# Two transformer-like layers on one core: turning the normalised x through DRAM instead of with ACT block copies

## The chip, the core and the metric

The kernel runs on one core of a Trainium2 chip. Its time is the device time of one execution in microseconds (us); of several runs the median is given. The engines are named as in the profile: PE (matrix multiply, with PEld for its weight loads), DVE (vector), ACT (activation), POOL (GpSimd) and SP, which here only issues DMAs.

## The reference

Everything is fp32. x has 2048 rows of 640 features. Two layers follow each other, each an attention block and a dense block, with shared weights:

```python
x = x + A(layernorm(x), wqkv, wo)          # twice, with B after each
x = x + B(layernorm(x), w1, b1, w2, b2)

def A(x, wqkv, wo):                        # 32 heads of 20, linear attention
    q, k, v = split(x @ wqkv)
    phi = lambda t: where(t > 0, t + 1, exp(t)) + 1e-6
    pq, pk = phi(q), phi(k)
    kv, z = einsum("bhsd,bhse->bhde", pk, v), pk.sum(over s)
    return ((pq @ kv) / (pq . z + 1e-6)) @ wo

def B(x, w1, b1, w2, b2):                  # 640 -> 1728 -> 640
    h = relu(x @ w1 + b1)
    return (h * h) @ w2 + b2
```

## The kernel before

The 2048 rows are 16 tiles of 128 rows (P = 128, 640 = D = 5 x 128, DC = 5). Each fp32 operand of a product is split into a high part, rounded by ACT, and a low part, the rest, made by DVE; a product is three matmuls (`mm3`). A matmul contracts over partitions, so the normalised x has to be turned: features onto partitions, rows along the free axis.

**The turn.** `blocks_T` (L370) transposes a 128 x 640 tile on DVE in 32 x 32 blocks, each block in its own place. `blocks_move` (L375) then moves the blocks to their places with 16 ACT copies of 32 partitions by 160 elements (L381). After that the tile is split into high (ACT) and low (DVE), by `xT_split` (L402, lines L130 and L131) in the attention block and by `x_split` (L1289, L1295 and L1297) in the dense block. The same two functions turn the attention's `pq` tiles (`b_ops`). Tiles 0, 1 and 2 of the first layer, and tiles 2 and 3 of each dense block, are turned by PE (`transpose5`).

**The attention loop** (L702) goes over the tiles t. Iteration t projects tile t to k and q (`part`), applies phi (`Phi`: ACT exp L491, DVE L498 and L499), gathers products of x and k of tile t - 1 (`g_part`, `gt_part`), normalises tile t + 2 (`a_apply`) and starts its turn, and splits tile t + 1. `k_post` makes the high and low parts of k (L683, L690) and adds k up on POOL (L687). In the first layer the loop also prepares w1 and w2 (`Prep`): it loads raw units (L265), splits them (L244, L248), and stores the split units to DRAM (L251); the wqkv split is stored as well (L210).

**The start of the first layer.** `FirstLoads` loads the k columns of wqkv in five chunks of 128 features, then the q columns in five more (L205), and splits them (L183 high, L189 low). Matmuls of the first tile (L726) follow chunk by chunk; the last of the q chunks stand in PE's order ahead of the first product of tile 1 (L395), and on ACT the splits of the last two q chunks stand ahead of the split of tile 1 (L130).

**The dense block** (from L1039) goes over four groups g of four tiles; in a group it goes over 14 chunks c of the 1728 hidden features. An iteration is `fc1` of chunk c (15 matmuls, L1064), `act` (ACT relu L1076, DVE L1077 to L1079), and `fc2` of chunk c - 1 (L1114). Beside it run, at places written out by hand, the attention outputs, norms and turns of the next group's tiles: `single` for tiles 4 to 7, `side` with the plans `fast(b)` for tiles 8 to 15. An event at (c, i) stands after tile i of `fc2` in iteration c, one at (c, "post") at the iteration's end. The split w1 and w2 units come back from DRAM through a ring of six buffers (`Units.load_ring`, L304). In the last group the next layer's tiles 0, 1 and 2 are normalised and turned (`side_last`).

**Order of the work.** The order on every engine is the program's order. All DMAs but one are issued by SP, in program order; an issue that waits holds up all behind it. SP's DMAs use eight completion semaphores in turn, so that a DMA is issued once the eighth before it has landed.

## Time and profile before

| | |
|---|---|
| time, median of 3 runs (lowest to highest) | 1351.68 us (1351.64 to 1351.83) |
| profiled execution | its time is its span, 1349.9 us; the page gives no other time for it |
| busy: PE, PEld, DVE, ACT, POOL | 1342.1, 1158.3, 911.7, 770.3, 123.4 us |
| DMA moved | 253.44 MB, mean 188 GB/s |

The span runs from the first instruction to the last; the timed runs hold 1.8 us more, which lies around it. A row of a group ends in "busy, mean of one in ns | idle time before, and what ended it". A row of the timeline begins with the start and the length in us.

### The profile page before, as it was taken

What the parts mean: (1) busy time and instruction counts of PE and PEld (TensorE: products, weight loads), DVE (VectorE), ACT (ScalarE), POOL (GpSimd) and SP (SyncE); (2) the same over time, 40 slices, a digit from 0 to 9 for tenths busy, and PEclk for the clock granted to TensorE, in tenths of its full rate; (3) what the DMA queues carried; (4) which work ended last, traced back from release to release, by engine and by line L of the source; (5) the groups of instructions that cost most, each with busy time, mean ns of one, the idle gap of its engine ahead of it and who ended that gap; (6) DMA issues with size and microseconds to landing.
All of it is one profiled execution on the core that took longest, in us unless ns stands there. A gap on an engine that the chain in (4) does not pass through costs nothing.

```text
span 1349.9 us, 18967 instructions
## 1 busy us (share of the span) xinstructions
PE 1342.1 (99%) x6797; PEld 1158.3 (86%) x6797; DVE 911.7 (68%) x1627; ACT 770.3 (57%) x1932; POOL 123.4 (9%) x174
## 2 busy tenths in 40 slices
PE   9999999999999999999999999999999999999998
PEld 8888998888888888888888899988888888888887
DVE  7888757777777676643467676677778667775323
ACT  5878858676546448411447688494756446464110
POOL 2222210000000000000012232100000000000000
PEclk9999999999999999999999999999999999999999
DMA  6787835574665475387521115156546646644734
GB/s 205 254 301 269 284 86 177 192 275 145 212 237 174 158 292 170 117 327 293 184 98 51 48 40 155 41 206 255 173 157 232 216 150 223 233 167 140 287 125 158
DMA packets 85635, 253.44 MB, mean 188 GB/s; under 512 B 11030, under 2 KB 19606, under 8 KB 84902
## 3 DMA queue, kind: packets, MB, share of 16 engines
q1 hardware_dynamic: 85398, 252.04, 53.7%
q8 instruction: 54, 0.88, 0.3%
q14 instruction: 39, 0.32, 0.1%
q10 hardware_dynamic: 144, 0.20, 0.0%
HBM read 193.50 MB, written 56.03 MB: 185 GB/s over the span
## 4 chain that ended last, share of the span: by engine, by line
PE 92%; DVE 3%; ACT 3%; DMA 1%; issue 1%; POOL 0%; SPq 0%; DVEq 0%; ACTq 0%
PE PS L395 34%; PE PS L1064 28%; PE PS L1114 28%; ACT z L381 2%; PE PS L911 1%; PE PS L924 1%; DMA st<-in_A_wqkv_dram 1%; PE PS L726 0%; DVE bn L352 0%; DVE xr L658 0%; DVE e L498 0%; DVE xTb L131 0%; DMA Mr<-Mc 0%; DVE r L499 0%; PE PS L1128 0%
## 5 line engine op out<-in xcount | busy, mean ns | idle before, releaser
L381 ACT ACTIVATE z<-y 32x160 f32<-32x160 f32 x1424 | 475.8, 334 | 75.2 <-DVE y L372 59.0
L1064 PE MATMUL PS<-xTb,u 128*128 128x512 f32 x1400 | 333.8, 390 | 1.0 <-DVE xTb L131 1.0
L1064 PEld LDWEIGHTS PS<-xTb,u 128*128 128x128 f32 x1400 | 261.6, 188 | 55.0 <-DVE xTb L131 1.5
L395 PE MATMUL PS<-kq,xT 128*128 128x320 f32 (+2 forms) x1575 | 284.4, 334 | 0.4 <-DVE GT L529 0.4
L1114 PE MATMUL PS<-u,h 128*128 128x512 f32 x1120 | 276.8, 390 | 0.0
L395 PEld LDWEIGHTS PS<-kq,xT 128*128 128x128 f32 x1575 | 250.1, 188 | 28.2 <-DVE rl L499 1.0
L1114 PEld LDWEIGHTS PS<-u,h 128*128 128x128 f32 x1120 | 208.5, 188 | 40.8
L1076 ACT ACTIVATE hr<-PS,b1sb 128x512 f32<-128x512 f32 x104 | 71.4, 687 | 297.6 <-PE PS L1064 296.9
L1077 DVE TENSOR_TENSOR hr<-hr 128x512 f32<-128x512 f32 x104 | 71.8, 690 | 217.4 <-ACT hr L1076 216.9
L395 PE MATMUL PS<-kh,xh 128*128 128x512 f32 x480 | 124.6, 393 | 0.0
L491 ACT ACTIVATE e<-PS 128x320 f32<-128x320 f32 (+4 forms) x128 | 53.5, 435 | 101.9 <-PE PS L395 93.5
L356 POOL TENSOR_SCALAR rs<-mv 128x1 f32<-128x1 f32 x64 | 28.0, 438 | 869.6 <-DVE mv L354 869.6
L395 PE MATMUL PS<-uM,pT 128*128 128x320 f32 x648 | 102.6, 309 | 0.7 <-DVE uM L940 0.7
L395 PEld LDWEIGHTS PS<-kh,xh 128*128 128x128 f32 x480 | 87.2, 188 | 15.6 <-DVE kh L690 0.4
L395 PEld LDWEIGHTS PS<-uM,pT 128*128 128x128 f32 x648 | 97.7, 188 | 3.1 <-DVE uM L940 1.2
L498 DVE TENSOR_SCALAR e<-e 128x320 f32<-128x320 f32 (+4 forms) x128 | 41.7, 325 | 80.0 <-ACT e L491 79.7
L1114 PE MATMUL PS<-h,u 128*128 128x512 f32 x280 | 79.0, 390 | 0.0
L1079 DVE TENSOR_TENSOR h<-hr,h 128x512 fp32r<-128x512 f32 x104 | 72.0, 693 | 3.6
L687 POOL TENSOR_TENSOR acc<-acc,r 128x640 f32<-128x640 f32 x30 | 53.8, 1795 | 198.5 <-DVE r L499 198.5
L1114 PEld LDWEIGHTS PS<-h,u 128*128 128x128 f32 x280 | 52.2, 188 | 10.8 <-DVE h L1090 0.4
L1064 PE MATMUL PS<-xTb,uw 128*128 128x512 f32 x240 | 57.0, 389 | 0.0
L499 DVE SCALAR_TENSOR_TENSOR r<-PS,e 128x512 f32<-128x512 f32 (+2 forms) x104 | 51.1, 492 | 5.8 <-ACT e L491 2.4
(126 smaller groups left out, 1353.9 us busy)
## 6 DMA issues: line engine op xcount, KB each, us to landing
u<-kept_w SPq DMA_DIRECT2D x184, 640.0 KB, 4.3
x<-x SPq DMA_DIRECT2D x48, 320.0 KB, 6.3
kept_w<-uprep SPq DMA_DIRECT2D x23, 640.0 KB, 4.9
pqt<-pq SPq DMA_DIRECT2D x32, 320.0 KB, 5.6
x<-xr SPq DMA_DIRECT2D x32, 320.0 KB, 2.4
st<-in_B_w_dram SPq DMA_DIRECT2D x22, 320.0 KB, 5.6
pq<-r SPq DMA_DIRECT2D x20, 320.0 KB
kept_kq<-kq SPq DMA_DIRECT2D x10, 640.0 KB, 5.7
```

The costliest lines, as they stand in the source:

```text
L356: nc.gpsimd.tensor_scalar(rs, mv[:, 1:2], LN_EPS, None, op0=ALU.add)
L381: nc.scalar.activation(zv[j * B32 : (j + 1) * B32, :, i, :], yv[i * B32 : (i + 1) * B32, :, j, :], AF.Copy)
L395: nc.tensor.matmul(ps, a, b, start=first and i == 0, stop=last and i == 2)
L491: nc.scalar.activation(self.e[:, a:b], ps, AF.Exp)
L498: nc.vector.tensor_scalar(e, e, 1.0, PHI_EPS, op0=ALU.min, op1=ALU.add)
L499: nc.vector.scalar_tensor_tensor(out=self.r[:, a:b], in0=ps, scalar=0.0, in1=e, op0=ALU.max, op1=ALU.add)
L687: nc.gpsimd.tensor_tensor(out=acc, in0=acc, in1=r, op=ALU.add)
L1064: nc.tensor.matmul(ps, a[:, d, :], bb[:, d, :], start=d == 0 and i == 0, stop=d == DC - 1 and i == len(seq) - 1,)
L1076: nc.scalar.activation(r, ps, AF.Relu, bias=b1sb[:, c : c + 1])
L1077: nc.vector.tensor_tensor(out=r, in0=r, in1=r, op=ALU.mult)
L1079: nc.vector.tensor_tensor(out=h[:, 1], in0=r, in1=h[:, 0].bitcast(F32), op=ALU.subtract)
L1114: nc.tensor.matmul(ps, l, r, start=first and k == 0, stop=last and k == len(a) - 1)
```

## The change

The turn of x now goes through DRAM. `spread` writes the normalised tile to DRAM with a DMA issued by POOL, and reads it back with four DMAs issued by SP: partition group j (32 partitions) of the tile `z` gets the features 160 j to 160 j + 159, in four blocks of 32 rows. One DVE transpose in 32 x 32 blocks (`turn`), with permuted access patterns, then gives the turned tile, and the 16 ACT copies go. Chunk c of the turned tile holds the features 160 j + 32 c + q on partition 32 j + q, no longer 128 c to 128 c + 127. So the rows of w1 and of wqkv's k and q columns are loaded in the same order, each load in four DMAs of 32 partitions; and where PE or ACT copies still turn x (the first three tiles of layer one, tiles 0 to 3 of each dense block) the normalised tile is written in permuted order. The attention's `pq` tiles keep their copies. In the dense block's plans some places move.

```diff
+JQ = P // B32
+Q = D // JQ
...
 def src_w1(c):
-            return [(v, w1[:, c * P : c * P + n].rearrange("(d p) f -> p d f", p=P))]
+            w = w1[:, c * P : c * P + n]
+            return [
+                (v[j * B32 : (j + 1) * B32], w[Q * j : Q * (j + 1)].rearrange("(d p) f -> p d f", p=B32))
+                for j in range(JQ)
+            ]
...
 class FirstLoads, step:
-                    nc.sync.dma_start(raw, wqkv[c * P : (c + 1) * P, D * (nm == "k") :][:, :D])
+                    for j in range(JQ):
+                        r = Q * j + B32 * c
+                        nc.sync.dma_start(
+                            raw[j * B32 : (j + 1) * B32], wqkv[r : r + B32, D * (nm == "k") :][:, :D]
+                        )
...
+    def spread(src):
+        n = bounce[0] % 8
+        bounce[0] += 1
+        d = dram.tile([P, D], F32, name="xb", tag=f"xb_{n}")
+        nc.gpsimd.dma_start(d, src)
+        z = ftile("z")
+        for j in range(JQ):
+            nc.sync.dma_start(
+                z[j * B32 : (j + 1) * B32].rearrange("p (i f) -> p i f", f=Q),
+                d[:, j * Q : (j + 1) * Q].rearrange("(i q) f -> q i f", q=B32),
+            )
+        return z
+
+    def turn(z):
+        y = ftile("y")
+        nc.vector.transpose(
+            out=y.rearrange("p (c i q) -> p i c q", c=DC, q=B32),
+            in_=z.rearrange("p (i c q) -> p i c q", c=DC, q=B32),
+        )
+        return y
...
 attention loop, iteration t:
-            move(t + 1)
             f.exp(0, ps)
...
                 a_apply(t + 2)
-                yza[t + 2] = blocks_T(xt[t + 2])
+                yza[t + 2] = spread(xt[t + 2])
             f.rest()
             ps = part(t, n0, D if is_late else 1024, bank(XB[1]))
             if t + 1 in yza:
-                xT_split(t + 1, yza.pop(t + 1)[1])
+                xT_split(t + 1, turn(yza.pop(t + 1)))
...
-            move(t + 2, AHEAD)
...
 x_split:
-            v = yzx.pop(t)[1].rearrange("p (c n) -> p c n", c=DC)
+            v = turn(yzx.pop(t)).rearrange("p (c n) -> p c n", c=DC)
...
 single:
-            at(b + 1, "post", lambda: blocks_move(yzx[t], (0, 1)))
+            at(b + 1, "post", lambda: x_spread(t))
-            at(b + 2, "pre", lambda: blocks_move(yzx[t], (2, 3)))
...
 fast(b), the entry "back": stats, apply, spread (moves before), split high, split low, bias
-        [((b, "post"), (b + 1, 0), (b + 1, 1), (b + 2, 0), (b + 2, 1), (b + 2, 3)),
-         ((b + 1, 3), (b + 1, "post"), (b + 2, 0), (b + 2, 4), (b + 3, 0), (b + 3, 1))],
+        [((b, "post"), (b + 1, 0), (b + 1, 2), (b + 2, 0), (b + 2, 1), (b + 2, 3)),
+         ((b + 1, 3), (b + 1, "post"), (b + 2, 0), (b + 3, 0), (b + 3, 1), (b + 3, 2))],
...
 side_last (next layer's tiles 0, 1, 2): spread at c = 7, 8, 11; turn and split of tiles 0, 1 at c = 9, 11
```

More of the change, by code (lines that the diff above doesn't have):

```diff
@@ L382, in blocks_move, with turn_move @@
                     zv[j * B32 : (j + 1) * B32, :, i, :], yv[i * B32 : (i + 1) * B32, :, j, :], AF.Copy
+                )
+    def turn_move(yz, js):
+        if len(yz) == 1:
+            yz.append(ftile("z"))
+        yv = yz[0].rearrange("p (j c q) -> p j c q", c=DC, q=B32)
+        zv = yz[1].rearrange("p (c i q) -> p c i q", c=DC, q=B32)
+        for j in js:
+            for i in range(P // B32):
+                nc.scalar.activation(
+                    zv[j * B32 : (j + 1) * B32, :, i, :], yv[i * B32 : (i + 1) * B32, j], AF.Copy
                 )
@@ L435, in a_stats, with a_apply @@
             ln_stats(("a", t), xt[t])
-    def a_apply(t):
-        if t < NT:
+    def a_apply(t, chunked=False):
+        if t < NT and chunked:
+            raw, xt[t] = xt[t], ftile("xp")
+            ln_apply(("a", t), by_chunk(xt[t]), by_block(raw))
+        elif t < NT:
             ln_apply(("a", t), xt[t], xt[t])
@@ L512, in split_new, with x_natural @@
             return u
+        def x_natural(t):
+            u = xtile("xh")
+            split(by_block(u[:, 0]), by_block(u[:, 1]), by_chunk(xt[t]))
+            return u
         def g_part(t, i):
@@ L787 @@
                 a_apply(3)
[L788 removed]
+                yza[3] = spread(xt[3])
             if early:
[L790 removed]
+                xT_split(2, turn(yz0[2]))
             for _ in range(PREP.get(t, 0) if layer == 0 else 0):
@@ L802 @@
                 fq.rest()
-            xh[t] = split_new(xt[t], "xh")
+            xh[t] = x_natural(t) if layer == 0 and t < 3 else split_new(xt[t], "xh")
             if gt and not is_late:
@@ L1006, in x_turned @@
             yzx[i] = blocks_T(xn.pop(i))
-            side_moves(yzx[i], lambda: f_split(i, yzx.pop(i)[1]))
+            side_work.extend(lambda k=k: turn_move(yzx[i], (k,)) for k in range(JQ))
+            side_work.append(lambda: f_split(i, yzx.pop(i)[1]))
         for i in range(2):
@@ L1470, in side @@
                 at(*ap_, lambda t=t: norm(t))
-                for k in range(4):
-                    at(s + (pl + k) // 5, (pl + k) % 5, lambda t=t, k=k: blocks_move(yzx[t], (k,)))
+                at(s, pl, lambda t=t: x_spread(t))
                 steps(at, lambda t=t: x_split(t), hi, lo)
```

55 lines of the change are left out of this document (26 added, 29 removed).

## The prediction

> **What bounds the kernel now.** I read the page first (busy times, chain, groups), then the waits, the DMA view, the start of the timeline, and windows and single lines of the stages that the change touches.
>
> ```profile
> span 1349.9 us, 18967 instructions
> PE 1342.1 (99%) x6797; PEld 1158.3 (86%) x6797; DVE 911.7 (68%) x1627; ACT 770.3 (57%) x1932; POOL 123.4 (9%) x174
> PE 92%; DVE 3%; ACT 3%; DMA 1%; issue 1%; POOL 0%; SPq 0%; DVEq 0%; ACTq 0%
> ...
> L381 ACT ACTIVATE z<-y 32x160 f32<-32x160 f32 x1424 | 475.8, 334 | 75.2 <-DVE y L372 59.0
> ```
>
> PE is busy for 1342.1 of 1349.9 us, and the chain that ended last is PE for 92%. The copies that go are ACT's largest group, but ACT is busy 57% of the span and holds 3% of the chain. So all of ACT's copies together can be worth no more than PE's idle time, 1349.9 - 1342.1 = 7.8 us, and of that only what waits for ACT. The waits of PE that the change could reach are small:
>
> ```profile
> PEld PS L1064 <- DVE xTb L131: 1.5, 2, 0.8
> PEld PS L924 <- ACT z L381: 0.9, 2, 0.4
> PEld PS L395 <- ACT kh L683: 0.8, 1, 0.8
> PEld PS L726 <- ACT kq L183: 0.6, 1, 0.6
> PEld PS L395 <- DVE kh L690: 0.4, 1, 0.4
> ```
>
> What can be lost is not limited in this way: PE's order is untouched, PE has no slack to give back, and whatever holds it up once is added to the end.
>
> **Removed.** 57 x tiles are turned by DVE and ACT before; 53 now go through DRAM (4, the first two of each dense block, keep the copies). That is 53 x 16 x 334 ns = 283 us less on ACT, all beside PE's work. The transposes of DVE stay in number. I cost this at nothing but the wait on L690 above: in iteration 1 of the first layer a DVE transpose stands ahead of it and goes, so 0.4 us are gained. The waits on L131 and on L381 (the pq copies) stay; the order ahead of them is as before.
>
> **The start: forty loads in place of ten.** This is the term that I expect to decide.
>
> ```profile
> 1.24 2.32 SPq L205 DMA_DIRECT2D st<-in_A_wqkv_dram  x5
> 3.60 0.43 SPq L431 DMA_DIRECT2D xt<-in_A_x_dram  x1
> 4.08 4.26 SPq L205 DMA_DIRECT2D st<-in_A_wqkv_dram  x5
> 14.65 1.37 ACT L183 ACTIVATE kq<-st 128x640 fp32r<-128x640 f32 x2
> 15.91 0.70 ACT L130 ACTIVATE xT<-PS 128x640 fp32r<-128x640 f32 x1
> 16.65 0.82 DVE L131 TENSOR_TENSOR xT<-PS,xT 128x640 fp32r<-128x640 f32 x1 [0.80 <-ACT xT L130]
> 17.31 3.70 PE L395 MATMUL PS<-kq,xT 128*128 128x512 f32 x15
> ```
>
> SP issues the first five chunks in 2.32 us. Now the DMA engines are what is late: in the window from 3 to 16 us they are full.
>
> ```profile
> 3.00:16.00 13.00, 12.62 (x77) 11.22 (x75) 10.44 (x19) 8.76 (x15) 4.00 (x8) 1.00 1.01 353
> ```
>
> The columns are length, busy time of PE, PEld, DVE, ACT and POOL, granted clock (1.00), DMA share (1.01) and GB/s (353). The last two chunks are split by ACT at 14.65 to 16.02, behind them ACT splits tile 1 (L130), DVE follows (L131), and PE's first long product stands at 17.31, from where it hardly stops. With the change each chunk is four DMAs of 80 KB, 40 chunk DMAs with tile 1's load between them, all on SP and in order. The last chunk DMA is the 41st, issued 40 pitches p after 1.24.
>
> The pitch of such a small DMA is not in the trace. Its bounds:
>
> ```profile
> 24.96 1.69 SPq L265 DMA_DIRECT2D st<-in_B_w_dram  x3
> 35.39 0.33 SPq L826 DMA_DIRECT2D pq<-r  x1
> L936 SPq DMA_DIRECT2D Mr<-Mc x8: 551/718/871, 215.3 to 889.0; - x8
> xt<-in_A_x_dram SPq DMA_DIRECT2D x16, 320.0 KB, 3.1
> out_dram<-x SPq DMA_DIRECT2D x15, 320.0 KB, 2.3
> ```
>
> From the start row one plain load takes 2.32 / 5 = 0.464 us. Two w1 loads (128 x 5 runs each) and one w2 load (128 runs) take 1.69 / 3 = 0.563 at 469 runs on average. So a run costs (0.563 - 0.464) / (469 - 128) = 0.00029 us, and a load of 32 runs, the nearest reading, 0.464 - 96 x 0.00029 = 0.44. I take p = 0.44. The low end is a lone issue (0.33) and the gap that the starts of the first rows show (3.60 - 1.24 - 2.32 = 0.04), 0.37; the high end is the M pieces (L936), the smallest transfers of the trace, 0.56 with that gap taken as nothing. The landing, from the issue's start: a 320 KB load takes 3.1 us; at 353 GB/s a quarter of its bytes saves 0.7, so 2.4, between 2.3 and 3.1.
>
> The last split then ends at 1.24 + 40 x 0.44 + 2.4 + 0.74 (half of 1.37, rounded up) = 22.0 instead of 16.02: **+6.0 us** on L130, L131 and the product at 17.31, since nothing of PE's order can go ahead of it. The ends: 1.24 + 14.8 + 2.3 + 0.74 = 19.1, +3.1; and 1.24 + 22.4 + 3.1 + 0.74 = 27.5, +11.5. SP's rule that the eighth DMA before must have landed asks for a landing under 8 p = 3.5 us, which holds at 2.4.
>
> The Trainium skill's page "DMA: Bandwidth & Descriptors", section "Rules for kernel authors", says to use one transfer over 128 partitions rather than two over parts of them, since the parts run on the same DMA engines one after the other. The same page, "Issuing engines are not separate DMA queues", calls the sequencer's time to initiate a DMA usually small relative to the DMA itself; by that rule the start would lose nothing (the first rival). This case's row has 0.464 us of issue beside 0.93 us of data (320 KB at 353 GB/s), so for a quarter of the data it is no longer small.
>
> **The detour itself, tile by tile.** Before, a tile had the time between its norm and ACT's split of the turned tile for the turn:
>
> ```profile
> 48.00 0.61 DVE L362 TENSOR_SCALAR xt<-xt,mv,rs 128x640 f32<-128x640 f32 x1
> 62.29 0.74 ACT L130 ACTIVATE xT<-z 128x640 fp32r<-128x640 f32 x1
> 395.21 0.60 DVE L362 TENSOR_SCALAR xn<-xr,mv,rs 128x640 f32<-128x640 f32 x1
> 402.88 0.73 ACT L1295 ACTIVATE xTb<-z 128x640 fp32r<-128x640 f32 x1
> 404.20 0.69 DVE L1079 TENSOR_TENSOR h<-hr,h 128x512 fp32r<-128x512 f32 x1
> 404.81 0.82 DVE L1297 TENSOR_TENSOR xTb<-z,xTb 128x640 fp32r<-128x640 f32 x1
> 410.40 0.69 DVE L1077 TENSOR_TENSOR hr<-hr 128x512 f32<-128x512 f32 x1 [2.44 <-ACT hr L1076]
> L687 POOL TENSOR_TENSOR acc<-acc,r 128x640 f32<-128x640 f32 x30 | 53.8, 1795 | 198.5 <-DVE r L499 198.5
> ```
>
> Now: POOL's issue (no POOL DMA is in the trace; between 0.33, SP's, and 1.8, POOL's one operation on a 128 x 640 tile, L687; I take 1.0, about midway, since neither row is near), its write to DRAM (2.3), four issues of SP (4 x 0.44 = 1.8), the last one's landing (2.4, less its issue): about 7.1 us, 6 to 9. In the attention loop 62.29 - 48.61 = 13.7 us are there. In the dense block, for the tighter tile of a pair, the new order puts DVE's `turn` behind L1079 of the next iteration, 404.89, so 404.89 - 395.81 = 9.1 us are there. Both hold. Behind `turn` in DVE's queue stand the low part (which now also waits for ACT's 0.73), the bias add and the next `act`: about 0.84 + 0.73 = 1.6 us, which the 2.44 us of idle time ahead of L1077 at 410.40 take up. No PE time.
>
> In the attention loop ACT's high part now stands behind DVE's `turn`, which stands behind L499, so the splits and exps after it come some 0.7 + 0.4 + 0.84 = 1.9 us later, and L690 by at most that. It was
>
> ```profile
> 46.25 0.77 DVE L690 TENSOR_TENSOR kh<-r,kh 128x640 fp32r<-128x640 f32 x1
> 48.95 1.29 PE L395 MATMUL PS<-kh,xh 128*128 128x512 f32 x5
> ```
>
> ready at 47.02 and used at 48.95: 1.9 us, just covered, and DVE is level again at the next exp, since the transpose that stood ahead of it is gone. Zero, with 0 to 1 us as bounds.
>
> SP gains queue. Its z reads wait for POOL's write, and the loads of raw w1 and w2, the stores of split units, the next tile's load and the stores of pq stand behind; in the dense block the unit loads do. A wait of some 4 us and four issues (1.8 us), with w1 loads at four issues, leaves a 12 us iteration room: pq 0.3, z 5.8, raw loads at most 9 x 0.44 = 4.0, x, stores and wqkv 5 x 0.45, in all 12.4 only while units come with two w1 each (twice), otherwise under 11. The raw units must be there for ACT's next splits:
>
> ```profile
> 62.93 1.98 ACT L244 ACTIVATE uprep<-st 128x640 fp32r<-128x640 f32 x3
> ```
>
> From the norm's end at 48.61: write landed at 51.9, z issued by 53.7, six to nine raw loads by 56.3 to 57.7, landed by 59 to 61, so 2 to 4 us are left. In the dense block a unit is loaded three iterations ahead and SP mostly waits for PE:
>
> ```profile
> SPq L304 <- PE PS L1114: 259.7, 61, 8.5
> ```
>
> so a load that comes 3 us late is hidden. Cost: zero, bounds 0 and 1 us.
>
> The sum, against the profiled execution: 1349.9 + 6.0 - 0.4 = 1355.5. The runs stand 1.8 us above the span, so 1351.7 + 5.6 = **1357.3 us**.
>
> **Rivals.**
>
> *The start loses nothing, and the rest is hidden: no change.* If an issue's time goes with its rows (0.464 / 4 = 0.12) the DMA engines stay the limit, the loads land as before, and only the 0.4 us are left: 1351.3. For it: the first five issues are back to back, so a limit on descriptors could set their pace. It decides if p is under 1.24 + 40 p + 3.1 = 16.0, p = 0.29. Against it: a lone issue takes 0.33 already, and the tiny M pieces no less than 0.55. 14%.
>
> *The attention loop of the first layer runs out of DMA.*
>
> ```profile
> 36.00:168.00 132.00, 131.99 (x705) 115.77 (x704) 110.59 (x205) 112.61 (x278) 33.57 (x33) 1.00 0.81 282
> ```
>
> The DMA engines are at 0.81 there, and 282 GB/s; the detour adds 0.655 MB for each of 11 tiles, 55 GB/s, to 337 of the 353 that the full start window reached. It decides when z or raw units come later than the 2 to 4 us above; a queue that costs 1.5 us in each of ten iterations gives 1357.3 + 15 = 1372. Against it: SP's wait for the write lets the queue drain once in each iteration. 12%.
>
> *POOL's DMA is slow.*
>
> ```profile
> L356 POOL TENSOR_SCALAR rs<-mv x64: 221/222/842, 5.0 to 1231.4; 128x1 f32<-128x1 f32 x64
> ```
>
> The same 128 x 1 step of POOL takes 221 ns alone and up to 842 ns beside DVE. If a POOL DMA is held up likewise, past the 9.1 us, DVE waits in the dense block with relu's successors behind it: 1 us more in each of the 8 tight tiles gives 1365. 8%. The Trainium skill's page "SBUF — State Buffer", section "Who interferes with whom", says that a DMA from GpSimd waits for its descriptors while DVE runs an operation that takes the port they share; no run here shows it yet for a DMA.
>
> *Faster.* If the start loses nothing and relief of ACT takes away PE's waits listed above (1.5 + 0.9 + 0.8 + 0.4 = 3.6, at most 3 of it), 1348.7. Against it: the releasers of the largest are DVE, behind unchanged PE work. 4%.
>
> **How the numbers follow.** Forecast 62%, and 14, 12, 8 and 4% for the rivals. The forecast's own range is 1351.7 + 3.1 - 0.4 = 1354.4 to 1351.7 + 11.5 - 0.4 = 1362.8. The range given, 1352.5 to 1371, reaches into the no-change case below and almost to the DMA case above. A change of 0.2% (2.7 us) is about what a measurement of this kernel can tell from none: the forecast's low end just reaches it. Faster 4%, same 14%, slower 82%.
>
> **What would show it.** Right: SP's issues at the start 0.4 to 0.5 us apart up to about 19 us, the DMA share of 3 to 16 us well under 1, the first product of tile 1 at about 23.3 instead of 17.31, and everything after it later by about the same 6 us, with PE's idle time after 25 us unchanged. Wrong: that product within 2 us of 17.31; or growing lag between 30 and 180 us with PE waits on xT or kh; or DVE waiting for z ahead of `turn` in the dense block by several us with PE waits on h.

## The result, and the profile after

The change makes the kernel slower: 1368.17 us (median of 4 runs, 1367.8 to 1371.52) against 1351.76 us of the kernel before on the same chip (4 runs, 1351.64 to 1351.88). The ratio is 1.0127, with a 95% interval of 1.0112 to 1.0141. The forecast was 1357.3, a loss of 5.6 us; 16.4 us were lost, nearly three times as much. The measured time lies in the range given only because that range reaches far beyond the forecast's own sum, which ended at 1362.8.

The profiled execution took 1367.84 us. The head of its page, with the shares of the chain that ended last:

```profile
span 1365.9 us, 18779 instructions
PE 1347.8 (99%) x6797; PEld 1161.5 (85%) x6797; DVE 911.4 (67%) x1627; ACT 493.4 (36%) x1084; POOL 156.2 (11%) x227
PE 84%; DVE 6%; DMA 3%; SPq 2%; ACT 2%; issue 1%; POOL 1%; DVEq 0%; ACTq 0%; POOLq 0%
```

The change does what it says: ACT is busy for 277 us less (770.3 before) with 848 instructions fewer. PE has the same 6797 matmuls, and the span is 16.0 us longer. The chain has moved from PE (92%) to DVE, DMA and SP's queue.

Since PE's order is the same in both traces, the n-th matmul of one can be set beside the n-th of the other. The lag is the difference of their ends. These are the places where it changes (start of PE's instruction in each trace, and the lag up to and with that place):

| place | before, us | after, us | lag after it, us |
|---|---|---|---|
| first product of tile 1 | 17.31 | 23.96 | 6.7 |
| layer-1 attention, iteration 1 (the product of kh, made by L690 / L757) | 34.76 | 41.12 | 6.3 |
| layer-1 attention, iteration 2 | 43.70 | 52.48 | 8.9, by 56 us 10.2 |
| layer-1 attention, tiles 11 to 15 | 134.22 to 180.17 | 145.32 to 194.56 | 14.4 |
| dense block 1, end of group 0 | 373.14 | 388.21 | 15.2 (14.5 just before) |
| dense block 2, end of group 0 | 1040.29 | 1056.24 | 16.1 (15.4 just before) |

Layer 2's attention adds nothing, and all else less than 0.4 us in all. **The start**, in the timeline of the kernel after (start, length; SP's issues, then ACT's last high part of wqkv, then PE):

```profile
1.25 9.23 SPq L212 DMA_DIRECT2D st<-in_A_wqkv_dram  x20
10.98 9.24 SPq L212 DMA_DIRECT2D st<-in_A_wqkv_dram  x20
21.82 0.74 ACT L188 ACTIVATE kq<-st 128x640 fp32r<-128x640 f32 x1 [0.96 <-DMA st<-in_A_wqkv_dram]
23.96 3.57 PE L448 MATMUL PS<-kq,xT 128*128 128x512 f32 x15
```

Twenty issues take 9.23 us, 0.46 us each, and ACT still waits for the last chunk. The window of 3 to 16 us, whose DMA share was 1.01 and rate 353 GB/s before, and the next six microseconds:

```profile
3.00:16.00 13.00, 8.89 (x50) 7.28 (x48) 7.88 (x15) 6.05 (x9) 1.77 (x4) 0.98 0.68 206
16.00:22.00 6.00, 5.86 (x23) 5.82 (x24) 3.00 (x4) 3.13 (x7) 1.50 (x5) 0.50 0.61 173
```

The DMA engines are only 0.68 busy: SP's queue is what is late.

**Layer-1 attention**, in windows of the kernel before and then of the kernel after (36 to 57 us holds iteration 2, 57 to 195 the rest):

```profile
36.00:57.00 21.00, 20.99 (x111) 17.96 (x110) 19.05 (x34) 18.22 (x43) 4.48 (x4) 1.00 0.82 262
57.00:195.00 138.00, 137.58 (x747) 121.88 (x746) 107.65 (x196) 108.58 (x268) 35.17 (x32) 1.00 0.71 246
```

```profile
36.00:57.00 21.00, 18.64 (x87) 15.66 (x86) 16.81 (x31) 6.64 (x12) 7.24 (x8) 0.92 0.74 198
57.00:195.00 138.00, 134.21 (x716) 117.19 (x715) 108.96 (x199) 52.80 (x95) 41.60 (x43) 1.00 0.93 315
```

ACT's busy time is halved or more, PE loses 2.4 and 3.4 us, and in the second window the DMA share rises from 0.71 to 0.93. How iteration 2 stalls is read in the timeline of the kernel after:

```profile
38.80 1.76 SPq L394 DMA_DIRECT2D z<-xb  x4
40.66 4.31 SPq L274 DMA_DIRECT2D st<-in_B_w_dram  x9
46.96 0.74 ACT L253 ACTIVATE uprep<-st 128x640 fp32r<-128x640 f32 x1 [1.32 <-DMA st<-in_B_w_dram]
49.41 0.74 ACT L253 ACTIVATE uprep<-st 128x640 fp32r<-128x640 f32 x1 [1.71 <-DMA st<-in_B_w_dram]
50.05 0.64 ACT L547 ACTIVATE e<-PS 128x128 f32<-128x128 f32 x2
52.48 1.60 PE L448 MATMUL PS<-xh,kh 128*128 128x320 f32 x6 [2.35 <-DVE r L555]
```

SP stands before the z reads until POOL's write has landed, at 38.80. Only then do three raw units go out, as nine transfers. Their split on ACT waits 1.32 and 1.71 us, the exp behind it comes at 50.05, phi's last step on DVE (L555) behind that, and PE waits 2.35 us for the PSUM bank (the piece of PE's output memory) that L555 has to read before PE may write it again.

The late tiles, for one of them from POOL's write to PE:

```profile
159.69 0.63 POOL L391 DMA_DIRECT2D xb<-xt  x1 [1.25 <-DVE e L554]
166.58 1.74 SPq L394 DMA_DIRECT2D z<-xb  x4
169.99 0.84 DVE L403 STREAM_TRANSPOSE y<-z 128x640 f32<-128x640 f32 x1 [0.33 <-DMA z<-xb]
173.88 0.88 DVE L590 TENSOR_TENSOR GT<-PS,GT 128x320 f32<-128x320 f32 x2
174.91 4.63 PE L448 MATMUL PS<-kq,xT 128*128 128x320 f32 x30 [1.11 <-DVE GT L590]
```

From issue to transpose it is 10.3 us, of which the write takes 6.9. The transpose waits 0.33 us for z; L590, which adds a PSUM bank to the running sum GT, comes later behind it and frees the bank late; and PE waits 1.11 us. In the last such tile the write took only 3.1 us, but the reads, issued at 182.68 behind four loads of wqkv, took until 189.65; DVE waited 2.30 us for them and PE behind it 1.81. In the waits between 30 and 200 us (total, times, longest) and in SP's own for the same stretch:

```profile
DVE y L403 <- DMA z<-xb: 4.8, 4, 2.3
PE PS L448 <- DVE GT L590: 2.9, 2, 1.8
PE PS L448 <- DVE r L555: 2.4, 1, 2.4
SPq L394 <- DMA xb<-xt: 37.4, 8, 7.3
```

### The profile page after: what moved, and what is told of

Read it like the earlier page. It is cut to its first block, busy times and chain, and to the rows that moved or that the text cites. A ratio compares the mean times of both kernels' runs of the same rounds, so it can differ in the third digit from the quotient of the medians.

```text
span 1365.9 us, 18779 instructions
## 1 busy us (share of the span) xinstructions
PE 1347.8 (99%) x6797; PEld 1161.5 (85%) x6797; DVE 911.4 (67%) x1627; ACT 493.4 (36%) x1084; POOL 156.2 (11%) x227
## 4 chain that ended last, share of the span: by engine, by line
PE 84%; DVE 6%; DMA 3%; SPq 2%; ACT 2%; issue 1%; POOL 1%; DVEq 0%; ACTq 0%; POOLq 0%
PE PS L448 30%; PE PS L1172 26%; PE PS L1122 26%; SPq L212 1%; PE PS L968 1%; PE PS L981 1%; ACT z L434 1%; DMA xb<-xt 1%; DMA st<-in_B_w_dram 1%; DVE bn L361 1%; DMA pq<-r 1%; DVE e L554 0%; DVE r L555 0%; DMA pqt<-pq 0%; DMA z<-xb 0%
## 5 line engine op out<-in xcount | busy, mean ns | idle before, releaser
L422 ACT ACTIVATE z<-y 32x160 f32<-32x160 f32 x512 | 171.1, 334 | 33.0 <-DVE y L413 21.6
L448 PEld LDWEIGHTS PS<-kh,xh 128*128 128x128 f32 x480 | 87.6, 189 | 16.4 <-DVE kh L757 1.2
L555 DVE SCALAR_TENSOR_TENSOR r<-PS,e 128x512 f32<-128x512 f32 (+2 forms) x104 | 51.1, 492 | 5.7 <-ACT e L547 1.5
```

Source lines behind the costliest of these rows:

```text
L422: nc.scalar.activation(zv[j * B32 : (j + 1) * B32, :, i, :], yv[i * B32 : (i + 1) * B32, :, j, :], AF.Copy)
L448: nc.tensor.matmul(ps, a, b, start=first and i == 0, stop=last and i == 2)
L555: nc.vector.scalar_tensor_tensor(out=self.r[:, a:b], in0=ps, scalar=0.0, in1=e, op0=ALU.max, op1=ALU.add)
```

## The experiments

My theory after the result had three parts: S, SP's forty issues hold the start; H and D, the wait for the DRAM write holds layer-1 attention, since it stands at the head of SP's queue (H) and makes z late (D); P, the transpose's new place on DVE costs in the dense blocks. Rivals were that the added DMA bytes do it, that the transpose's place on DVE does it in attention too (O), and that POOL's DMA is slow (W). Each run's own kernel before is the base of its difference.

### The start

**e1.** The kernel before, with quarters alone:

```diff
-                    nc.sync.dma_start(raw, wqkv[c * P : (c + 1) * P, ...])
+                    for j in range(4):      # rows c * P + 32 j, in their old order
+                        nc.sync.dma_start(raw[j * B32 : (j + 1) * B32], wqkv[r : r + B32, ...])
```

> The kernel before with one edit: each of the ten first loads of wq and wk goes as four transfers of 32 rows (rows in their old order, nothing else changed). Theory S (the start is held by the number of issues on SP's queue): forty issues 0.46 us apart, the product of tile 1 at 23 to 24 us instead of 17.31, and the whole run later by as much, 6.0 to 6.7 us: 1358 (1357 to 1359). Rival (the start's loss comes from the normalised x being written in chunks, or from the order of the copies on ACT, not from the loads): product of tile 1 within 1 us of 17.31, time 1352 to 1353.

1358.30 us, +6.44; ratio 1.0048 (1.0033 to 1.0063). Timeline and window of this kernel:

```profile
10.99 9.24 SPq L207 DMA_DIRECT2D st<-in_A_wqkv_dram  x20
23.62 3.91 PE L399 MATMUL PS<-kq,xT 128*128 128x512 f32 x15
```

```profile
16.00:22.00 6.00, 5.05 (x29) 4.09 (x29) 3.25 (x5) 3.15 (x7) 2.85 (x6) 1.00 0.62 180
```

The quarters alone are the whole of the start's loss, and nothing is added later (lag 6.56 at the product, 6.66 at the end). The granted clock is 1.00 here from 16 to 22 us, and it was 0.50 in the kernel after; the product stands at 23.62 and 23.96. So the half clock cost some 0.3 us at most at the start: PE waited for data anyway.

**e13.** The same with two transfers of 64 rows.

> The kernel before with one edit: each of the ten first loads goes as two transfers of 64 rows (with four of 32 rows it was 6.5 us slower). Theory S (one queue issues a transfer every 0.46 us, whatever its size, and this holds the start): twenty issues take 9.3 us for the same bytes, 164 KB in 0.46 us is 353 GB/s, about what the engines move at the start of the kernel before (321 to 401): product of tile 1 at 17.3 to 18.5, time 1351.7 to 1353. Rival (the loss goes with the count of transfers or with the rows in each, by landing and not by issue): half of the loss, product of tile 1 at 20 to 21, time 1354.5 to 1355.5.

1356.42, +4.44; ratio 1.0033 (1.002 to 1.0046); the product at 21.01. Both readings miss, S the more:

```profile
1.24 6.33 SPq L207 DMA_DIRECT2D st<-in_A_wqkv_dram  x10
```

```profile
3.00:16.00 13.00, 10.27 (x56) 8.84 (x54) 8.43 (x16) 6.88 (x10) 2.51 (x5) 1.00 0.98 250
```

Ten issues take 6.33 us, 0.63 each and not 0.46, one behind the other from the first on: an issue does not cost the same whatever its size. At 160 KB in 0.63 us SP hands out 260 GB/s; the DMA engines are full as well, 0.98, at 250 GB/s instead of 353. So halves move slower than whole transfers, and this run does not tell whether SP or the engines set the pace. The Trainium skill's page "SBUF — State Buffer", section "Door 1: The DMA port swizzle", says that a transfer of 64 partitions reaches no more of the memory's ports than one of 32, half of them; the drop from 353 to 250 GB/s agrees in direction, and no run here separates the ports from another cause.

**e2.** The kernel after, with one transfer for each first load whose source has four runs of 32 rows:

```diff
-                    for j in range(JQ):
-                        r = Q * j + B32 * c
-                        nc.sync.dma_start(raw[j * B32 : (j + 1) * B32], wqkv[r : r + B32, ...])
+                    w = wqkv[...].rearrange("(j c i) n -> c j i n", j=JQ, c=DC)
+                    nc.sync.dma_start(raw, w[c])
```

> The changed kernel with one edit: each first load is again one transfer of 128 partitions, with a source of four runs of 32 rows, so the features stand as in the changed kernel and only the count of transfers falls, from forty to ten. Theory S: the start's lag of 6.65 us goes but for the ACT table load behind the first wait (about 1 us) : product of tile 1 at 17.3 to 18.5, time 1361 to 1363. Rival (a source in four pieces lands as slowly as four transfers, the DMA engines and not SP hold the start): product of tile 1 at 22 us or later, time 1366 to 1368. Second rival (the later stalls near 52 us and from 134 to 181 us come from the late start itself): they change too, and the time falls below 1360.

1387.60, +35.7: far worse, beyond the first rival. Since the start came later still, this run does not test the second rival; e5 and e6 do, which keep the late start and lose the stalls. A window of this kernel, and PE at the product of tile 1:

```profile
18.00:22.00 4.00, 1.97 (x6) 1.56 (x6) 0.82 (x1) 1.45 (x2) 0.00 (x0) 0.50 0.26 99
```

```profile
43.13 5.14 PE L445 MATMUL PS<-kq,xT 128*128 128x512 f32 x14
```

The DMA engines are 0.26 busy, four of sixteen, at 99 GB/s. The Trainium skill states this rule on its page "DMA: Bandwidth & Descriptors", section "Why a DMA increments its semaphore by 16 and not by 1": the number of engines is the largest, up to 16, that divides the outermost dimension of both sides. An outermost 4 gives four, and the trace agrees.

**e7.** The quarters shared out over three queues:

```diff
+                        q = (nc.sync, nc.sync, nc.scalar if nm == "k" else nc.gpsimd, nc.gpsimd)[j]
-                        nc.sync.dma_start(
+                        q.dma_start(
```

> The changed kernel with one edit: of the four transfers of each first load two are issued by SP, and the others by ACT and POOL (wk) or by POOL alone (wq). Theory S (0.46 us per issue on one queue holds the start, at 0.61 to 0.74 of the DMA engines' time): 20 issues on SP take 9.3 us, the engines come to 0.9 or more, product of tile 1 at 18 to 20 us, and the time falls by 4 to 6 us, to 1362 to 1364. Rival (transfers of 32 rows move at 200 GB/s from any number of queues): product of tile 1 at 23 to 24 us, time 1367 to 1369. Second rival: the issues of ACT and POOL are so late behind their own work that wk chunks arrive later than now: over 24 us, time 1369 or more.

1368.85 (1366.24 to 1371.68), +17.0: nothing gained, and the product of tile 1 stands at 23.46, both as the first rival has it, but not for its reason.

```profile
3.00:16.00 13.00, 11.06 (x55) 9.98 (x54) 8.60 (x17) 6.62 (x10) 7.67 (x16) 0.87 1.05 268
```

```profile
15.64 1.09 POOL L213 DMA_DIRECT2D st<-in_A_wqkv_dram  x2
21.54 0.74 ACT L188 ACTIVATE kq<-st 128x640 fp32r<-128x640 f32 x1 [2.79 <-issue]
```

With three queues the engines are full (1.05), at 268 GB/s, and the loads do gain: up to the last q chunk the lag is 3.4 us, where the kernel after has 6.7. The last chunk gives it away. Two of its quarters are issued by POOL only at 15.64, behind POOL's part of the norm of tile 1; they land at 21.47, ACT splits the chunk at 21.54, and the lag at the product is 6.2. That is the mechanism of the second rival, for wq and not for wk. So S is right for one queue. What the start would lose with the last chunk in time, no run shows; the lag of 3.4 here and of 3.7 in e13, both with full engines at 250 to 270 GB/s, suggests that transfers to parts of the partitions would lose some of it still.

### Layer-1 attention

**e5.** The reads into z take the same blocks from x and wait for nothing:

```diff
-                d[:, j * Q : (j + 1) * Q].rearrange("(i q) f -> q i f", q=B32),
+                xf[t * P : (t + 1) * P, j * Q : (j + 1) * Q].rearrange("(i q) f -> q i f", q=B32),
```

> The changed kernel with one edit: the four reads that fill z take the same 32-row blocks from the input x (always tile 0) in place of the DRAM tile just written, so they wait for no write; the write itself stays. Left out: the turned x is not the normalised one. All instructions, bytes and transfers are as before the edit. Theory D (z's late arrival is the cause of the stalls after the start: the reads wait 3 to 8 us at the head of SP's queue for POOL's write, raw units queue behind them, and the transpose waits up to 2.3 us for z): the stall at 52.5 us goes (3.9 us), and the waits on GT and kh between 134 and 181 us (4.2 us) shrink to under 1 us; lag at the first fc1 7 instead of 14.4, time 1360 to 1361. Theory O (the transposes' place in DVE's order is the cause): the waits on GT of 1.2 to 1.6 us stay, time 1364 to 1365. Either way the start's 6.65 us stays.

1360.23, +8.37; ratio 1.0063 (1.0048 to 1.0078). That is 7.9 us less than the kernel after. Windows and waits (30 to 200 us) of this kernel:

```profile
57.00:195.00 138.00, 137.38 (x742) 121.28 (x742) 111.18 (x202) 54.61 (x98) 43.05 (x43) 1.00 0.93 311
```

```profile
PE PS L448 <- DVE GT L590: 0.6, 1, 0.6
```

D holds. The DMA engines are as full as in the kernel after (0.93, 311 GB/s), and PE still gets its 137.4 us. So the bytes by themselves are not the price; the wait of the reads for the write is, with all that is late behind it. The transpose stands in the same place on DVE, so O's waits should have stayed; 0.6 us of them did.

**e6.** Attention as before, everything else as after (`blocks_T` and `turn_move` in place of `spread` and `turn` in the loop).

> The changed kernel with the detour undone in the attention loops alone (tiles 2 to 15 of a layer are transposed by DVE from SBUF and moved by 16 ACT copies, at the old places, with the new order of features); start, w1 loads and the dense blocks stay changed. If the growth from 41 to 195 us belongs to the detour in layer-1 attention: lag at the first fc1 6.3 to 7.3, the dense 1.6 us stay, time 1359 to 1361. Rival (the raw units' nine issues or the chunked order of x cost as much by themselves): 1363 or more. Second rival (layer-2 attention gained from the detour and loses that now): more than 1 us of new lag between 660 and 900 us.

1360.01, +8.15. Attention's detour costs 8.2 us, as e5 says in another way, and the lag at 180 us is 6.6, the start's. Layer 2's attention neither gained nor lost.

**e9.** The reads issued behind the raw loads:

```diff
-                yza[t + 2] = spread(xt[t + 2])
+                yza[t + 2] = spread(xt[t + 2], late_reads)     # the write alone
...
                 prep.load()
+            for d in late_reads:                               # the four reads
+                yza[...] = spread_reads(d)
```

> The changed kernel with one edit: in the attention loops the four reads into z are issued behind the iteration's raw loads and no longer ahead of them; POOL's write stays where it is, and so does the transpose. Theory H (the wait for the write at the head of SP's queue holds back the raw units and all that is queued there; that is what costs 3.9 us near 52 us): this stall falls to under 1 us, and as the write has landed by the time the reads reach the head, z comes hardly later; the late tiles (165 to 195 us, where z itself is late by up to 2.3 us) stay as they are or grow by 1 us. Time 1364 to 1366. Rival (z's own lateness is the price everywhere, so that reads issued later only make it later): stall near 52 us unchanged or grown, more waits of DVE for z: 1369 to 1375.

1363.21 (1362.45 to 1365.69), 5 us better, and a little better than H expected. SP and ACT in the timeline of this kernel:

```profile
31.62 4.26 SPq L274 DMA_DIRECT2D st<-in_B_w_dram  x9
39.72 1.74 SPq L400 DMA_DIRECT2D z<-xb  x4
45.02 1.98 ACT L253 ACTIVATE uprep<-st 128x640 fp32r<-128x640 f32 x3
```

The nine raw transfers no longer stand behind the wait, ACT's three splits run without a pause, and the stall of iteration 2 is gone (lag 6.2 to 6.5 up to the late tiles). Two waits on GT remain, 3.3 us in all and 3.0 us of lag, where z is late itself. So H is the price near 52 us and D in the late tiles.

**e4.** Raw units of w1 as single transfers, three issues instead of nine.

> The changed kernel with one edit: each raw unit of w1 is again one transfer (its rows in the old order, so fc1's weights do not match the turned x in this run). Three raw units are then 3 issues instead of 9 in one iteration of layer-1 attention. Theory Q (the stall of PE at 52.5 us, 3.9 us with the half clock behind it, comes from raw units that land late behind the z reads and nine issues on SP): they land about 2.7 us sooner, the wait for the bank at 52.5 us falls below 1 us, time 1364 to 1366. Rival (z's wait at the head of SP's queue alone makes them late, or ACT is late for another reason): the stall at 52.5 us stays within 0.5 us of 2.35, time 1367 to 1368.5.

1366.68 (1364.61 to 1368.35). The stall at 52.5 us goes here too (lag 6.8 there), so it needed both the wait and the nine issues. But the late tiles took more: `PE PS L444 <- DVE GT L586` is 4.8 us where it was 2.9. PE came to them 3 us earlier, and the longest wait for z is 3.9 us there, after 2.3. The profiled execution is the slowest of the four, and 1.4 us of its lag come from the wait for z near 1140 us that is told under e11.

**e3.** The transpose moved ahead on DVE:

```diff
                 yza[t + 2] = spread(xt[t + 2])
+            if t + 1 in yza:
+                yza[t + 1] = turn(yza[t + 1])
             f.rest()
...
-                xT_split(t + 1, turn(yza.pop(t + 1)))
+                xT_split(t + 1, yza.pop(t + 1))
```

> The changed kernel with one edit: in layer-1 and layer-2 attention the DVE transpose of tile t+1 stands where the old one stood, ahead of the second phi pass of the same iteration, and only the split stays where it was. Theory O (the late tiles lose 4.2 us because the transpose stands on DVE ahead of the addition that frees the PSUM bank, L590, or ahead of kh): the waits of PE on GT and kh between 134 and 181 us shrink to under 1 us together, time 1364 (1363 to 1366). Rival D (z comes late, as its write and its reads take up to 7 us): DVE now waits for z in the earlier place, the phi passes behind it are late, PE waits for r or kh instead, time 1368 or more, up to 1375.

1366.38 (1365.97 to 1369.26), between the two readings. The stall near 52 us stayed. The waits between 30 and 200 us show what became of the rest:

```profile
DVE y L403 <- DMA z<-xb: 11.6, 6, 4.8
PE PS L448 <- DVE r L555: 5.2, 3, 2.5
PE PS L448 <- DVE GT L590: 0.9, 2, 0.8
```

The waits on GT fell from 2.9 to 0.9 us as O expects, and the waits on phi's last step rose from 2.4 to 5.2, since DVE now stands 11.6 us for z. That is D's mechanism, in an execution that is the slowest of the four by 2.8 us.

**e8.** `nc.gpsimd.dma_start(d, src)` in `spread` becomes `nc.sync.dma_start(d, src)`.

> The changed kernel with one edit: the write of the normalised tile to DRAM is issued by SP and not by POOL. Theory W (the 3.3 to 8 us from issue to landing belong to POOL's queue): landing falls to 2 to 3 us, z comes 3 to 4 us sooner, the stall at 52.5 us halves and the waits for z between 165 and 190 us go: 1363 to 1366. Rival L (the DMA engines are full between 57 and 190 us, 0.82 to 1.0 busy, so any write waits behind the loads and stores already queued): landing still 4 to 8 us, and now SP's queue also stands before the write until DVE has normalised the tile: 1368 to 1372.

1411.09, +59: worse than both readings. SP's own waits from 30 to 200 us in this kernel:

```profile
SPq L394 <- DMA xb<-xt: 58.4, 11, 7.3
SPq L391 <- DVE e L554: 6.2, 3, 4.4
```

SP waits 5.3 us on average (58.4 / 11) and up to 7.3 for the write to land, so W falls: POOL's queue is not what makes it slow. In the kernel after it lands in 2.6 to 2.7 us at 36 and 411 us, and in 3.1 to 7.8 us between 42 and 190 us, where the DMA engines are 0.93 busy. The load on the engines is the likely reason. Layer 2's attention makes the same round trip without the loads of w1 and w2: between 700 and 850 us the engines are 0.36 busy, 13 writes land in 2.5 to 3.8 us, and the lag does not grow.

### The dense blocks, and versions put together

**e11.** The order of features put into the tile that goes to DRAM, and not into the weights' rows:

```diff
-            ln_apply(("a", t), by_chunk(xt[t]), by_block(raw))
+            ln_apply(("a", t), by_block(xt[t]), by_chunk(raw))     # tiles that are spread
-            split(by_block(u[:, 0]), by_block(u[:, 1]), by_chunk(xt[t]))
+            split(by_chunk(u[:, 0]), by_chunk(u[:, 1]), by_block(xt[t]))
```

> The detour kept, but the permuted order put into the normalised tile that is written to DRAM (the normalisation writes it in blocks, the natural copy of x reads it back in order) instead of into the rows of the weights: first loads and raw units of w1 are single transfers again, as in the kernel before, and the start is the old code. Theory S+H: the start's 6.65 us go, of the 3.9 us near 52 us some 3 go as in the run with single w1 transfers, the 2 to 4 us of the late tiles and the 1.6 us in the dense blocks stay: 1356 to 1359. Rival (the writes and reads of the normalised tile in pieces of 32 elements make DVE's instructions dearer, 0.6 to 0.8 us each, on thirteen tiles a layer): 1360 or more.

1359.66 (1358.35 to 1360.29), at the edge of both. The start is free (lag 0 to -0.2), attention leaves a lag of 4.7, the dense blocks add some 0.8 twice, and a wait for z of 2.25 us in the second dense block at 1142 us adds 2.2. In the profiled execution of the kernel after z came there in time; in those of e4, e7 and e10 DVE waits 1.3 to 1.5 us at the same place and PE loses 1.2 to 1.4. So the dense block's time for the detour is not always enough either. Such differences may be why the runs of most versions with the wait spread by 2 to 5 us and those of e5 by 0.1; no run isolates it.

**e10.** The dense transpose behind the fourth output product instead of at the unit's end.

> The changed kernel with one edit: for the four single tiles of the first dense group the DVE transpose is issued behind the fourth output product of fc2 instead of behind the whole unit, some 1 to 4 us sooner, apart from the split that follows it. Theory P (the 0.8 us of lag at 373 us and again at 1040 us come from the 0.84 us transpose and the wait of 0.81 us for ACT that stand on DVE in the last unit of that group, ahead of the additions that free PSUM): both go, 1366.4 to 1367. Rival (they come from something else in that stretch, such as DVE's work for the pairs): 1368 as now, or later if DVE waits for z at the new place.

1368.66 (1366.81 to 1370.1): no change, and the steps of lag at the end of group 0 stayed (0.7 and 0.6 us, as in the kernel after). The reason is in DVE's timeline at the end of group 0, in the kernel before, then after:

```profile
358.69 0.84 DVE L372 STREAM_TRANSPOSE y<-pqt 128x640 f32<-128x640 f32 x1
359.46 0.78 DVE L1297 TENSOR_TENSOR xTb<-z,xTb 128x640 fp32r<-128x640 f32 x1
361.11 0.68 DVE L1085 TENSOR_TENSOR hr<-PS,hr 64x512 f32<-64x512 f32 x1 [0.86 <-ACT hr L1084]
```

```profile
373.24 0.85 DVE L413 STREAM_TRANSPOSE y<-pqt 128x640 f32<-128x640 f32 x1
374.01 0.80 DVE L403 STREAM_TRANSPOSE y<-z 128x640 f32<-128x640 f32 x1
375.62 0.82 DVE L1355 TENSOR_TENSOR xTb<-y,xTb 128x640 fp32r<-128x640 f32 x1 [0.81 <-ACT xTb L1353]
376.36 0.68 DVE L1143 TENSOR_TENSOR hr<-PS,hr 64x512 f32<-64x512 f32 x1
388.21 2.11 PE L1172 MATMUL PS<-u,h 128*128 128x512 f32 x8 [0.37 <-DVE x L1197]
```

Before, one operation of 0.78 us stood there, and DVE then had 0.86 us to spare. After, it is transpose, wait for ACT, and low part: 0.80 + 0.81 + 0.82 = 2.43. The difference, 1.65, less the 0.86 to spare, is 0.79, close to the step of 0.7 that PE shows there. From there DVE has no pause up to the additions L1197. In e10 the transpose ran from 373.79, still right ahead of its low part and behind the same work, so DVE waited the same 0.81 us.

**e14.** e11 with e9's order of reads, and the dense low part one unit later (`(b + 3, 0)` for the second place of `x_split`).

> The run with the order put in by the normalisation, with two edits more: in attention the reads into z are issued behind the iteration's raw loads, and in the dense blocks the low part of a single tile's split is issued one unit later than its high part, so that DVE does not stand 0.81 us waiting for ACT. Theory H and P together: the lag that run had by 135 us (1.7) goes, that of the late tiles (3 us at 162 and 180 us) goes to 2 to 3, the two steps of 0.84 us at 373 and 1040 us go: 1353.5 to 1356. Rival (the steps at 373 and 1040 us come from something else): they stay, 1355 to 1357.5.

1359.21 (1357.95 to 1361.08), above both readings. Attention's lag fell to 2.2. But the second edit was a mistake: DVE's low part ran at 366.83 to 367.66, and the next group's first product, which reads it, stood until 367.76; 1.8 us of lag at 364 us and again at 1031, in place of some 0.8 each.

**e15.** e14, with each attention tile normalised and sent at the end of the iteration before.

> The same with one edit more: each attention tile is normalised and sent to DRAM at the end of the iteration before, some 3 us sooner. Theory D for the late tiles (their loss is z's late arrival: normalised tile to transpose takes 10 to 11 us, where the short iterations have 10.5): waits of DVE for z and of PE for GT near 162 and 180 us go to under 0.5 us each, lag at the first fc1 under 1 us, time 1351 to 1353. Rival O (the transpose and its wait for ACT stand ahead of GT's addition on DVE): the waits on GT of 1.2 to 1.6 us stay at 162 and 180 us, time 1353.5 to 1356.

1358.72 (1358.43 to 1359.37), above both readings, with e14's 1.8 us in each dense block still in it. It gained little: DVE still waits 1.8 us for z in one late tile and 2.8 in another, where the reads stand among loads of wqkv and wo, and the longest wait on GT is 2.3. So the remedy failed, since z was late again; between D and O this run does not decide.

**e16.** e14 with the dense split placed anew, `steps(at, x_split, (b + 2, 0), (b + 2, "post"))`.

> The run with the order put in by the normalisation, with the reads into z behind the raw loads (attention), and in the dense blocks, for the four single tiles, the transpose and the high part of the split issued behind the first output product of the unit and the low part at its end, as in the changed kernel, so that work of DVE that stood ahead of the transpose (reciprocal, product, transpose of another tile: 2.0 us) now lies between the high and the low part. Theory P (DVE stood 0.81 us for ACT between transpose and low part, and the 0.84 us transpose came late, in the one unit whose end the additions L1185 wait for): the steps of 0.84 us at 373 and 1040 us go to 0.2 or less; with the lag of about 2.2 us after attention the time is 1353.5 to 1355. Rival (z comes too late for the earlier place, and DVE waits for it there): steps of 0.8 us or more stay, 1355 to 1358.

1356.36 (1355.13 to 1357.67), above the range. DVE in this kernel:

```profile
361.58 0.84 DVE L401 STREAM_TRANSPOSE y<-z 128x640 f32<-128x640 f32 x1
363.77 0.84 DVE L411 STREAM_TRANSPOSE y<-pqt 128x640 f32<-128x640 f32 x1
364.54 0.78 DVE L1354 TENSOR_TENSOR xTb<-y,xTb 128x640 fp32r<-128x640 f32 x1
```

Other work lies between transpose and low part, the wait for ACT is gone, and of the lag that the two dense blocks add 0.5 us in all is left: P holds. The time is high since a wait of 1.98 us on GT at 182.9 us was followed by half clock (0.72 in the mean of 182 to 188 us), 4.3 us of lag after attention instead of 2.2.

**e12.** e11's order, with the detour in the dense blocks and layer 2's first three tiles alone, and e10's place.

> As the run with the order put in by the normalisation, but with the detour in the dense blocks and for the first three tiles of layer 2 alone (attention loops of the kernel before, blocks moved by ACT), and with the transpose of the single tiles issued earlier. By the parts measured so far nothing of the loss is left (start 0, attention 0, dense 0 to 0.8): 1351.5 to 1352.7, the same as before within 0.2% while some 280 us of ACT work in all, or most of it, are gone. Rival (ACT's copies did cost something in the dense blocks, and it shows now): under 1350. Second rival (the dense 1.6 us come back through the strided normalisation on DVE): 1353 to 1354.

1352.70 (11 runs, 1352.1 to 1353.22); ratio 1.0008 (0.9999 to 1.0017). What is left are the two steps, some 0.65 us each.

**e17.** The same with e16's place.

> The run with the detour in the dense blocks alone, with the place of the split mended as in the last run (transpose and high part behind the first output product, low part at the unit's end). Theory P, if it covers all that is left: the steps at 373 and 1040 us (0.6 and 0.8 us in the run that only moved the transpose) go, and the time comes to 1351.0 to 1351.9, the same as before with some 140 us less work on ACT. Rival (the detour's transfers, 0.56 of the DMA engines against 0.52 between 200 and 1340 us, cost something on their own): 1352.3 to 1353.

1351.60 us (11 runs, 1350.94 to 1351.89) against 1351.61; ratio 0.9999 (0.999 to 1.0008). Its page:

```profile
PE 1342.0 (99%) x6797; PEld 1158.8 (86%) x6797; DVE 910.7 (67%) x1627; ACT 629.4 (47%) x1500; POOL 140.6 (10%) x201
```

141 us less on ACT than in the kernel before, and the same time. No step is left in its lag (within 0.1 us from 20 us to the end). That closes the dense term: all of it was the split's place. It also answers what the dense blocks' copies were worth: nothing. No version beats the kernel before.

## Why the prediction was wrong

- **Bound and removed work: right.** PE is the bound, and 277 us fewer on ACT (283 were worked out) gave back only the wait on L690: the lag falls by 0.3 us there, and in e6, which keeps attention's copies, it does not.
- **Start: right.** +6.0 were forecast (3.1 to 11.5) and the product at about 23.3; it came at 23.96, +6.65. The pitch was 0.46 instead of 0.44. e1 gives 6.44 us for this term alone. The pitch is not the same for every size, though: halves were issued 0.63 apart (e13). The rule quoted from the Trainium skill's page "DMA: Bandwidth & Descriptors", section "Issuing engines are not separate DMA queues", that an issue is usually small beside its transfer, doesn't hold here: 80 KB in 0.46 us left the engines 0.68 busy. The rule of one transfer over 128 partitions (the Trainium skill, same page, "Rules for kernel authors") held: quarters cost 6.44 us, halves 4.44.
- **Detour, tile by tile: the landing of the write was mis-sized.** The step took 2.3 us, from stores to DRAM in quiet stretches; in layer-1 attention it was 3.1 to 7.8. So 7.1 us became 10.3 to 11.4 in the last three tiles, from POOL's issue to the transpose. The 13.7 us were read from an early iteration; in these three only 9.1 to 10.0 us lie between POOL's issue and the transpose's place on DVE (as 169.99 - 0.33 - 159.69).
- **SP's queue and attention's order: the step that failed. It was priced at zero, with 0 to 1 us as bounds; it cost 7.9 us (e5), 8.2 (e6).** The raw units had "2 to 4 us" to spare; they came 3 us too late in iteration 2, by the write's wait and the nine issues together (e9, e4). I followed that only to kh (L690) and not to the PSUM bank, which phi's last step holds, and in the late tiles not to the bank that the addition on GT holds.
- **Dense: priced at zero, 1.7 us.** The tile looked at was one of a pair, with 2.44 us of idle time behind it. The tile that counts is the last single one, with 0.86, in the unit whose end PE waits for. e16 and e17 show that it was the place alone.
- **Rivals.** The one of attention running out of DMA was the right place and mechanism in part ("when z or raw units come later than the 2 to 4 us"), but it was set against the forecast, not added to it, and for the wrong reason: e5 carries the same bytes without loss. POOL's DMA was slow to land but not as POOL's (e8); POOL's issue itself took 0.54 to 0.78 us throughout, with DVE busy for 0.67 of the span.
- **The sum by the runs:** 6.44 (e1) + 7.94 (e5) + 1.7 (the dense blocks, 14.4 to 16.1 of lag) = 16.1, of 16.4 measured.

## What to carry to other kernels

A round trip through DRAM costs its two latencies in series, and the wait between them stands on the queue that issues the second half: price it by who is queued behind it, with the landing time of the busiest stretch, and put it behind the loads that others need. In a kernel whose bound engine has no slack, read the slack of every moved step at its tightest place (the shortest iteration, the unit before a group's end), and ask which PSUM bank or buffer the delayed engine holds, not only which operand it makes. Fewer instructions on an engine that is off the chain are worth nothing, here 141 us for nothing at all, and splitting loads to reorder rows was paid in full; let an engine that passes over the data anyway write the order instead.

## What the runs showed of the hardware

- In the window of 3 to 16 us, mostly loads of wqkv, the DMA engines moved 353 GB/s in transfers of 128 partitions (1.01 busy), 250 in halves (0.98), 206 in quarters from one queue (0.68) and 268 in quarters from three (1.05).
- SP issued these loads 0.46 us apart in transfers of 128 and of 32 partitions (2.32 us for five, 9.23 for twenty), and 0.63 apart in transfers of 64 (6.33 for ten).
- A source with four outer runs kept the transfer on 0.26 of the DMA engines, 99 GB/s.
- A write of 320 KB to DRAM landed 2.5 to 3.8 us after its issue where the engines were 0.36 busy (layer 2's attention) and 3.1 to 7.8 us after it where they were 0.93 busy, issued by POOL; issued by SP it was as slow (waits of up to 7.3 us).
- After a wait of 2.35 us PE ran with a granted clock of 0.50 from 54 to 56 us, which cost 1.3 us more of lag; at the start the same clock cost some 0.3 at most. The Trainium skill's page "TensorE: Matmul & The Clock Gate", section "What's actually happening", gives windows of some 3.4 us for this; here shorter waits were enough, and not always: with a wait of 2.04 us that ended at 16.14 us the clock of the kernel after fell (0.50 from 16 to 22 us), and with one of 2.06 that ended at 16.18 in e1 it stayed at 1.00.
